# Attention and a channel-mix layer on one core: when the second stage's weights are loaded, and in which memory

## The chip, the core and the metric

One core of one Trainium2 chip runs the kernel. The metric is the device time of one execution in microseconds (us). PE is TensorE (matmul), DVE is VectorE, ACT is ScalarE, POOL is GpSimd, and SP only issues transfers (DMAs); ACT issues some as well. A difference of 0.2% is about what a measurement of this kernel can tell from none.

## The reference, cut to what matters

```python
scores = 30 * tanh((q @ k.T) / sqrt(64) / 30)          # 8 batches x 12 heads, 448 x 64
attn   = softmax(scores) @ v                            # -> x: 8 x 448 x 768
xk = mu_k * x + (1 - mu_k) * x_prev                     # x_prev: the token before
xr = mu_r * x + (1 - mu_r) * x_prev
k  = maximum(xk @ w_k, 0)                               # 768 -> 1024, "the keys"
out = sigmoid(xr @ w_r) * ((k * k) @ w_v)               # 768 -> 768, 1024 -> 768
```

Everything is float32. A float32 product is made of three matmuls of a faster type: each operand is split into a high part (a copy in that type) and a low part (the operand less its high part).

## The kernel before

**First stage.** Two heads are a pair; 48 pairs, six to a batch. For each pair PE makes the scores, ACT takes tanh and exp, DVE sums the rows, PE multiplies by v. The row sums go to DRAM and back (`gather`, `recip`, `rec_store`, `rec_load`), then DVE normalizes (`norm`, L382), and DVE, ACT and POOL make xk and its high and low parts (`x_high`, `x_low`). The keys of a batch are 8 columns of w_k (`fc`) by 6 pairs (`dc`) by 3 matmuls = 144 matmuls of 448 columns, dealt out among the later pairs' work (`K`). From pair 14 on two pairs make one `unit`, and the string `UNIT` lists in which order the program writes out their work. Each engine takes its own instructions in that order.

**The passage.** After the last pairs, 36 key matmuls of batch 6 and all 144 of batch 7 are left. The pools of attention are closed, and seven weight groups are prepared: `group_load` reads two blocks of w_r or w_v from DRAM into a staging tile (`stg`, two buffers), `group_sums` makes four sums and differences of their quarters (POOL, but group 0 on DVE), `group_split` makes the high part of seven quarters by ACT (L107, 2688 columns) and the low part by DVE (L577), and then loads the group after next. `TAIL` says which of this follows which eighth of batch 7's keys. Two banks hold the keys on their way from PE to `relu` (ACT, L454). The mixing of xr (`mix_r`, L615 and L616) and its first sum (`sum1`, L634) follow the keys.

**Second stage.** 14 blocks of 256 tokens, each a run `r` and a run `v`, each run seven products of a Strassen-like scheme (L661; 9 matmuls of 384 columns in `r`, 12 in `v`). A table of slots (`PRODUCTS`, `runs`) interleaves them: the first is r's product 4, then r's 2, 3 and 0, then v's 4, then r's 5. Product 3 adds to the bank of product 4, after ACT has copied that bank out (L672).

Of the kernel before, what the change touches and what calls it, by code (L numbers as in the profile page):

```python
# [19 lines left out]
DF = 1024  # L20
# [36 lines left out]
TAIL = ("d0 s0", "p1", "s1 p2", "s2", "p3", "s3 p4", "s4 p5", "p6")  # L57
# [20 lines left out]
k_store k_store f x_high.1 x_low.1 weight_store load_vl load_v.1 x_store.0 weight_load load_qk.1 x_store.1"""  # L78

# [9 lines left out]
class Body:  # L89
# [26 lines left out]
    def consts(self, pool):  # L116
        nc = self.nc
        self.cap_t = pool.tile([P, 1], F32, name="cap_t")
        nc.sync.dma_start(self.cap_t, self.cap.to_broadcast([P, 1]))
        self.scl_t = pool.tile([P, 1], F32, name="scl_t")  # L120
        nc.vector.reciprocal(self.scl_t, self.cap_t)
        nc.vector.tensor_scalar(self.scl_t, self.scl_t, D ** -0.5, None, op0=ALU.mult)
        self.mu, self.om = {}, {}
        for n, src in (("k", self.muk), ("r", self.mur)):
            m = pool.tile([P, ND], F32, name="mu_" + n)
            nc.sync.dma_start(m, src)
            o = pool.tile([P, ND], F32, name="om_" + n)
            nc.vector.tensor_scalar(o, m, -1.0, 1.0, op0=ALU.mult, op1=ALU.add)
            self.mu[n], self.om[n] = m, o
        self.grd = pool.tile([P, 1], F32, name="grd")  # L130
        if self.maxima:
            nc.vector.memset(self.grd, 1e-9)
            return
        sq = pool.tile([1, 1], F32, name="sq")
# [37 lines left out]
    def init_attn(self):  # L172
        self.raw, self.QK, self.rawv, self.S, self.P32, self.PV, self.R, self.rs = ({} for _ in range(8))
        self.M, self.SUM = {}, {}
        self.one = self.rawp.tile([P, 64], F32, name="one", bufs=1)
        self.nc.gpsimd.memset(self.one, 1.0 / 32)
# [9 lines left out]
    def load_v(self, i):  # L186
        t = self.rawv[i] = self.rawp.tile([P, 3, 2, D], F32, name="rv")
        w = 6 * D
        self.nc.sync.dma_start(t.rearrange("p c h d -> p (c h d)"),
                               self.v[i // NP, i % NP // 2][:, i % 2 * w:i % 2 * w + w])  # L190

    def load_vl(self, i):
        t = self.rawv[i, "L"] = self.rawp.tile([P, 2, D], F32, name="rvl")
        self.nc.sync.dma_start(t.rearrange("p h d -> p (h d)"), self.v[i // NP, i % NP // 2][:, 12 * D:])
# [361 lines left out]
    def group_load(self, k):  # L556
        p, g = self.group(k)
        c = g if p == "r" else ND + g
        w = self.stg.tile([P, 7, HN], F32, name="stg", tag=f"stg{k % 2}")
        for j in range(2):  # L560
            self.nc.sync.dma_start(w[:, 2 * j:2 * j + 2].rearrange("p a e -> p (a e)"), self.w_d[c + j * KG[p]])
        self.W[k] = w
# [10 lines left out]
    def group_split(self, k):  # L573
        p, g = self.group(k)
        w, (hi, lo) = self.W.pop(k), self.WS[p, g]
# [5 lines left out]
    def weight_tiles(self, pool, p, gs):  # L581
        w = pool.tile([P, len(gs), 2, 7, HN], F32R, name="w2" + p, align_bytes=256)
        for j, g in enumerate(gs):
            self.WS[p, g] = w[:, j, 0], w[:, j, 1]

    def tail_work(self, h):
        for op in TAIL[h].split():
            if op[0] in "dp":
                self.group_sums(int(op[1]), "v" if op[0] == "d" else "p")
            else:  # L590
                self.group_split(int(op[1]))


    def load_x(self, c):
# [3 lines left out]
        xc = self.XC = self.xin.tile([P, ND, CH + 2], F32, name="xc")  # L598
# [46 lines left out]
    def split(self, p, c, m):  # L645
        a = self.block(p, c, m)
        hi, lo = (self.opp[p].tile([P, KG[p], P], F32R, name=p + t, align_bytes=256) for t in "hl")
# [64 lines left out]
    def chain(self, pe, prep, s0, s1):  # L712

        for s in range(s0, s1):
            if s in pe:
                self.product(*pe[s])
            for fn, a in prep.pop(s, []):
                fn(*a)
# [3 lines left out]
    def step(self, i):  # L722
# [19 lines left out]
        for op in (UNIT if unit else START_EVEN if even else START_ODD).split():  # L742
            g, j1 = (), 0
            if "." in op:
                op, j1 = op[:-2], int(op[-1])
            if op[-1] in "012L" and op not in ("L", "VL", "OL"):
                op, g = op[:-1], (op[-1] if op[-1] == "L" else int(op[-1]),)
            if op in pair:
# [14 lines left out]
                if 0 <= j < NPAIR and op not in (late if j in ONES else first) and not (uncut(j) and op in ('qk_high', 'qk_low')):  # L763
                    getattr(self, name.get(op, op))(j, *g)
            elif op == "K":
# [27 lines left out]
    def run(self):  # L793
# [8 lines left out]
        with ExitStack() as outer:  # L802
# [10 lines left out]
            kst, hst, est, wst, ast, sst, pst = (ExitStack() for _ in range(7))  # L813
# [4 lines left out]
            self.WKH, self.WKL = ([w.tile([P, ND, DF // 2], F32R, name=n, align_bytes=256) for w in (wk0, wk1)]  # L818
                                  for n in ("wkh", "wkl"))
            self.ps_k = pool("ps_k", 2, pst, space=PSUM)  # L820
# [3 lines left out]
            sump = pool("sump", 1, ast, **right)  # L824
            self.up = pool("up", 2, ast, **right)
            self.rawp = pool("rawp", 2, ast, **right)
            self.qp = pool("qp", 3, ast, **right)
# [3 lines left out]

            self.init_x(self.up)
# [8 lines left out]
            for i in range(NSTEP):  # L841
# [4 lines left out]
                if i == NPAIR + 1:  # L846
# [4 lines left out]
                    for st in (wst, est, ast, sst, pst):  # L851
                        st.close()
                    self.W, self.WS, self.A, self.S1, self.OP, self.bank, self.RS = ({} for _ in range(7))
                    self.weight_tiles(pool("w2r", 1, **right), "r", range(3))
                    self.opp = {"r": pool("opr", 3, **right)}
                    self.xin = pool("xin", 1, **right)
                    self.stg = pool("stg", 1, **right)
# [4 lines left out]
                    self.ps_k = pool("ps_k", 2, pst, space=PSUM)  # L862
                    self.ps_2 = pool("ps_2", 1, space=PSUM, **right)
                if i <= NPAIR:
                    self.step(i)
                if i > NPAIR + 1:
                    for h in range(2):
                        n = B * NF * ND * 3 - (2 * (NSTEP - i) - h) * 3 * ND
# [3 lines left out]
                        h += 2 * (i - NPAIR - 2)  # L872
                        if h == 4:
                            hst.close()
                            self.weight_tiles(pool("w2v0", 1, **right), "v", range(2))
                        self.tail_work(h)
# [5 lines left out]
            self.weight_tiles(pool("w2v1", 1), "v", range(2, 4))  # L882
            self.rsp, self.opp["v"] = pool("rsp", 1), pool("opv", 3)
            self.chain(pe, prep, -12, -6)
            self.group_split(6)
            self.CP = self.stg.tile([P, 7, HN], F32, name="cp", tag="stg0")
            self.chain(pe, prep, -6, -3)
            self.group_split(5)
            t = self.stg.tile([P, 7 * HN], F32, name="x1", tag="stg1")
            self.kr1 = t[:, 0:NF * CH].rearrange("p (c s) -> p c s", c=NF)  # L890
            self.S1["v"] = t[:, NF * CH:NF * CH + KG["v"] * P].rearrange("p (c s) -> p c s", c=KG["v"])
            self.chain(pe, prep, -3, max(pe) + 1)
# [52 lines left out]
```

## Time and profile before

| | us |
|---|---|
| median of 3 runs | 942.55 (941.82 to 942.9) |
| the profiled execution | 943.12 |
| its span | 941.3 |
| PE busy | 893.2 (95%) |
| DVE, ACT, POOL busy | 733.2, 620.8, 423.4 |

A span is cut in windows, and each window lists how long each engine was busy in it, and the clock that PE was granted (1.00 is 2.4 GHz, 0.50 is 1.2 GHz). A timeline row is a start, a duration, an engine with the line, what is written from what, and in brackets the idle time before it and the engine that ended it. PE's rows overlap their successors, so the distance between starts is what a matmul costs.

### The profile page before, as it was taken

How to read it: one execution, taken by the hardware profiler on the slowest of the kernel's cores; microseconds unless marked ns; L12 is line 12 of the kernel's file. 1: busy time of each engine (PE TensorE's matmuls, PEld its weight loads, DVE VectorE, ACT ScalarE, POOL GpSimd, SP SyncE). 2: the span in 40 equal slices, each digit the busy share in tenths (PEclk: the TensorE clock that was granted, in tenths of full speed). 3: DMA queues.
4: the chain of work that ended last, by engine and by line, in shares of the span. 5: the costliest groups of instructions: out<-in, count | busy, mean ns of one | idle time of the engine just before them, and what ended most of it. 6: DMA issues, size and time to landing. Idle time of an engine off the chain costs nothing.

```text
span 941.3 us, 14302 instructions
## 1 busy us (share of the span) xinstructions
PE 893.2 (95%) x5046; PEld 700.4 (74%) x5046; DVE 733.2 (78%) x1088; ACT 620.8 (66%) x957; POOL 423.4 (45%) x412
## 2 busy tenths in 40 slices
PE   7999999999999999999999638999999999999996
PEld 2334556667777676777669538999999999999996
DVE  5778997777888888878874368888888888888873
ACT  7888878787887887877863346554554555555542
POOL 2433364456556546455534853333433334333440
PEclk9999999999999999999999959999999999999999
DMA  7446655657776656666638422323332233323301
GB/s 249 122 150 183 193 172 171 185 164 200 216 207 195 196 172 187 204 207 195 183 111 274 142 77 88 104 80 111 104 113 93 80 104 113 105 88 102 113 26 46
DMA packets 96410, 137.06 MB, mean 146 GB/s; under 512 B 11464, under 2 KB 84936, under 8 KB 96328
## 3 DMA queue, kind: packets, MB, share of 16 engines
q1 hardware_dynamic: 87112, 121.37, 42.1%
q10 hardware_dynamic: 9216, 14.68, 4.2%
q8 instruction: 41, 0.67, 0.3%
q14 instruction: 41, 0.34, 0.1%
HBM read 91.23 MB, written 42.38 MB: 142 GB/s over the span
## 4 chain that ended last, share of the span: by engine, by line
PE 50%; DVE 22%; ACT 13%; issue 7%; DMA 4%; POOL 3%; SPq 1%; ACTq 0%; POOLq 0%; DVEq 0%
PE kps L444 20%; PE pv L285 11%; PE s L250 10%; DVE vl L649 3%; DVE cp L692 3%; DVE t L616 3%; ACT vh L107 3%; DVE rl L649 3%; PE ps2a L661 2%; PE pv L294 2%; PE s L260 2%; ACT t L615 2%; ACT rh L107 2%; DVE x L621 2%; DVE kr L621 2%
## 5 line engine op out<-in xcount | busy, mean ns | idle before, releaser
L266 ACT ACTIVATE p<-s,scl_t 128x896 f32<-128x896 f32 x144 | 139.2, 996 | 16.0 <-PE s L250 14.8
L444 PE MATMUL kps<-xkh,wkl 128*128 128x448 f32 x384 | 144.4, 376 | 4.1 <-ACT ko L454 4.1
L276 ACT ACTIVATE p<-p,cap_t 128x896 f32<-128x896 f32 x144 | 145.2, 1036 | 1.9
L331 DVE TRANSPOSE_TENSOR_REDUCE r<-p 128x28 f32<-128x896 f32 x126 | 136.2, 1093 | 7.6 <-ACT p L276 7.6
L444 PE MATMUL kps<-xkl,wkh 128*128 128x448 f32 x384 | 141.4, 368 | 0.0
L444 PE MATMUL kps<-xkh,wkh 128*128 128x448 f32 x384 | 141.1, 368 | 0.0
L526 POOL TENSOR_TENSOR wsq<-wa,wsq 128x384 f32<-128x384 f32 x44 | 47.1, 1071 | 157.6 <-DVE wsq L519 157.6
L285 PE MATMUL pv<-p,rv 128*64 128x448 f32 x576 | 115.1, 545 | 0.0
L661 PE MATMUL ps2a<-w2v,vh 128*128 128x384 f32 x448 | 88.5, 339 | 8.3 <-DVE cp L691 8.3
L444 PEld LDWEIGHTS kps<-xkh,wkl 128*128 128x128 f32 x384 | 72.1, 188 | 30.8 <-issue 13.7
L285 PEld LDWEIGHTS pv<-p,rv 128*64 128x64 f32 x576 | 38.6, 136 | 66.5 <-issue 55.8
L661 PEld LDWEIGHTS ps2a<-w2v,vh 128*128 128x128 f32 x448 | 77.8, 188 | 13.0 <-DVE cp L691 11.0
L444 PEld LDWEIGHTS kps<-xkl,wkh 128*128 128x128 f32 x384 | 72.2, 188 | 9.1 <-issue 2.8
L444 PEld LDWEIGHTS kps<-xkh,wkh 128*128 128x128 f32 x384 | 72.1, 188 | 6.5
L382 DVE TENSOR_TENSOR x<-pv,r 128x448 f32<-128x448 f32 x48 | 28.2, 620 | 55.0 <-DMA r<-rec_d 54.8
L649 DVE TENSOR_TENSOR rl<-t,rh 128x384 fp32r<-128x384 f32 x70 | 39.7, 567 | 39.1 <-ACT rh L107 38.2
L113 POOL TENSOR_TENSOR qkl<-rqk,qkh 128x832 fp32r<-128x832 f32 x34 | 67.5, 1986 | 2.7
L661 PE MATMUL ps2a<-w2r,rh 128*128 128x384 f32 x336 | 68.2, 338 | 0.2 <-ACT rh L107 0.2
L649 DVE TENSOR_TENSOR vl<-x,vh 128x512 fp32r<-128x512 f32 x63 | 56.1, 898 | 13.9 <-ACT vh L107 13.7
L661 PEld LDWEIGHTS ps2a<-w2r,rh 128*128 128x128 f32 x336 | 59.7, 190 | 0.8 <-ACT rh L107 0.8
L616 DVE SCALAR_TENSOR_TENSOR t<-xc,mu_r,t 128x256 f32<-128x256 f32 (+3 forms) x120 | 56.8, 526 | 1.1 <-ACT t L615 0.3
L113 POOL TENSOR_TENSOR xkl<-xk,xkh 128x448 fp32r<-128x448 f32 x48 | 55.3, 1152 | 3.9
(125 smaller groups left out, 1903.5 us busy)
## 6 DMA issues: line engine op xcount, KB each, us to landing
rqk<-qk SPq DMA_DIRECT2D x47, 448.0 KB
k_d<-ko ACTq DMA_DIRECT2D x64, 224.0 KB
x_d<-x SPq DMA_DIRECT2D x48, 224.5 KB
out<-cp SPq DMA_DIRECT2D x56, 192.0 KB
rv<-v SPq DMA_DIRECT2D x48, 192.0 KB
r<-rec_d SPq DMA_DIRECT2D x36, 224.0 KB
kr<-k_d SPq DMA_DIRECT2D x7, 1024.0 KB
x<-k_d SPq DMA_DIRECT2D x7, 1024.0 KB
```

Source lines behind the costliest of these rows:

```text
L107: self.nc.scalar.copy(out, x)
L113: {"p": self.nc.gpsimd, "v": self.nc.vector}[e].tensor_sub(*a)
L250: nc.tensor.matmul(s[:, h, 0:S], qk[a][p, k], qk[b][p, 0:S], start=(n == 0), stop=(n == len(terms) - 1))
L266: self.nc.scalar.activation(p32, self.S.pop((i, g))[:, :, 0:S], AF.Tanh, scale=self.scl_t)
L276: self.nc.scalar.activation(p32, p32, AF.Exp, scale=1.0 if self.maxima else self.cap_t)
L285: nc.tensor.matmul(pv[p, 0:S], v[:, g, h, :], ph[:, h, :], start=(g == 0), stop=False)
L331: self.nc.vector.tensor_reduce(out=r1[:, :, 3 if g == "L" else g], in_=self.P32[i, g].rearrange("p h (b k) -> p (h b) k", k=32), axis=mybi ...
L444: nc.tensor.matmul(self.kps[fc][:, 0:S], w, m[:, dc, :], start=first, stop=last)
L526: {"p": self.nc.gpsimd, "v": self.nc.vector}[e].tensor_add(sq, f(a), sq)
L616: nc.vector.scalar_tensor_tensor(out=td, in0=self.XC[:, d, j0 + o + 1:j1 + o + 1], scalar=self.mu["r"][:, d:d + 1], in1=td, op0=ALU.mult, ...
L649: self.nc.vector.tensor_sub(lo, a, f(hi))
L661: self.nc.tensor.matmul(o, a[:, g], self.WS[p, g][w][:, m], start=first and part == 0 and g == 0, stop=last and part == 2 and g == KG[p] - ...
```

## The change

Attention's tiles and those that live longer now stand in separate pools (`ast`, `lst`); the first is closed inside the last unit, right after its last matmuls with v, and the tiles of the second stage (`w2A` to `w2O`, one of 10.5 KB per partition each) wait for the old tiles that they lie on, one by one. Groups 0, 1 and 2 are loaded, summed and split within the last unit (`LAST`, in which `l`, `p` or `d`, `c`, `s` are load, sums on POOL or DVE, high, low). A low part goes into a slot whose raw group is done with. `mix_r` and `sum1` of the first block move among batch 7's keys (`@` in `TAIL`). Batch 7's first four columns take pairs 0 to 3 first and pairs 4 and 5 later, and each of its eight columns has a bank of its own. The tile sizes and two pads put every tile of the first stage on a multiple of 64 bytes; in the program before most lay 32 bytes off.

```diff
-TAIL = ("d0 s0", "p1", "s1 p2", "s2", "p3", "s3 p4", "s4 p5", "p6")
+TAIL = ("p3 s2 @-12 @-11 @-10", "p4 c3 s3", "p5 @-9", "open c4 s4 @-8 c5", "p6", "@-7 @-6", "@-5 @-4", "")
+TAIL_TAGS = ("c0", "b0", "a0", "c1", "b1", "a1")
+LAST = """V.0 V.1 VL next gather f f f p0 recip weight_load rec_store f f weight_rest weight_sum rec_load l2 d1 c0 s0
+norm.0 norm.1 K K K relu K relu k_store c1 mix_old.0 mix_new.0 x_high.0 x_low.0 s1 weight_low f K K mix_old.1 relu
...
@@ key_order
+        if b == B - 1:
+            early = [x for x in t[:4 * n] if x[1] < 4]
+            return early + [x for x in t[:4 * n] if x[1] >= 4] + t[4 * n:]
@@ kpart
-                if self.ps_k is not None:
+                if self.ps_2 is not None and fc > 1:
+                    self.kps[fc] = self.ps_2.tile([P, 512], F32, name="kps", tag="ps2" + TAIL_TAGS[fc - 2])
+                elif self.ps_k is not None:
@@ group_split
-        self.copy("s", hi, w)
-        self.nc.vector.tensor_sub(lo, w, f(hi))
-        if k + 2 < KG["r"] + KG["v"]:
-            self.group_load(k + 2)
+    def group_high(self, k):
+        hi = self.weight_tile(HIGH[k], F32R)
+        self.WS[self.group(k)] = [hi, None]
+        self.copy("s", hi, self.W[k])
+    def group_low(self, k):
+        pair = self.WS[self.group(k)]
+        pair[1] = self.weight_tile(LOW[k], F32R)
+        self.nc.vector.tensor_sub(pair[1], self.W.pop(k), f(pair[0]))
@@ run
+            def open_first():
+                ast.close()
+                self.weight_slots(pool("w2a", 1, **tile_wise), "EGDFHBCA")
+                for k in range(2):
+                    self.group_load(k)
...
-                    for k in range(2):
+                    for k in (3, 5):
                         self.group_load(k)
-                    pe, prep = self.runs()
-                    self.chain(pe, prep, -40, -12)
+                    self.preps(-23)
+                    self.group_load(4)
+                    self.preps(-16)
...
-            self.chain(pe, prep, -12, -6)
-            self.group_split(6)
...
+            self.tail_work("s5 c6")
+            self.chain(pe, -6, -1)
+            self.prep[-1].reverse()
+            self.preps(-1)
+            self.tail_work("s6")
```

On SP, from the last stores of x of the unit before to the last weight load: `sq<-r` is the gather of the row sums, `r<-rec_d` the return of the reciprocals, `xc` and `kr` the second stage's x and keys. Before:

```order
L361 DMA sq_171<-r_170 32x224 x4
L373 DMA rec_d_88<-rs_5110 28x2x32
L378 DMA r<-rec_d_88 64x2x448 x2
L546 DMA w_d<-wsq 128x384
L415 DMA x_d<-x_140 128x449
L415 DMA x_d<-x_142 128x449
L561 DMA stg<-w_d 128x768 x4
L599 DMA xc<-x_d 128x6x257
L603 DMA kr<-k_d 128x8x256
L561 DMA stg<-w_d 128x768 x10
```

Now:

```order
L576 DMA w2A<-w_d 128x768 x2
L576 DMA w2C<-w_d 128x768 x2
L371 DMA sq_179<-r_178 32x224 x4
L383 DMA rec_d_88<-rs_5160 28x2x32
L388 DMA r<-rec_d_88 64x2x448 x2
L576 DMA w2E<-w_d 128x768 x2
L561 DMA w_d<-wsq 128x384
L425 DMA x_d<-x_147 128x449
L425 DMA x_d<-x_149 128x449
L576 DMA w2I<-w_d 128x768 x2
L576 DMA w2H<-w_d 128x768 x2
L634 DMA xc<-x_d 128x6x257
```

Groups 0 and 1 now stand ahead of the gather, and group 2 right behind the return; groups 4 and 6 (`w2K`, `w2M`) and two more loads follow these rows.

On POOL, the last pairs' x parts, the weight sums (`stg`) and the first block's sums (`s`). Before:

```order
L526 TENSOR_TENSOR wsq<-wa,wsq 128x384
L103 TENSOR_SCALAR xkh<-xk 128x448
L113 TENSOR_TENSOR xkl<-xk,xkh 128x448
L103 TENSOR_SCALAR xkh<-xk 128x448
L113 TENSOR_TENSOR xkl<-xk,xkh 128x448
L113 TENSOR_TENSOR stg<-stg 128x384 x24
L879 TENSOR_LOAD flag
L634 TENSOR_TENSOR s_5510<-t 128x384
```

Now:

```order
L122 TENSOR_TENSOR w2A<-w2A 128x384 x4
L541 TENSOR_TENSOR wsq<-wa,wsq 128x384
L112 TENSOR_SCALAR xkh<-xk 128x448
L122 TENSOR_TENSOR xkl<-xk,xkh 128x448
L112 TENSOR_SCALAR xkh<-xk 128x448
L122 TENSOR_TENSOR xkl<-xk,xkh 128x448
L122 TENSOR_TENSOR w2I<-w2I 128x384 x4
L122 TENSOR_TENSOR w2K<-w2K 128x384 x4
L122 TENSOR_TENSOR w2H<-w2H 128x384 x4
L669 TENSOR_TENSOR s_5374<-t 128x384
L122 TENSOR_TENSOR w2M<-w2M 128x384 x4
L122 TENSOR_TENSOR s_5374<-s_5374,t 128x384
```

Twelve weight sums instead of 24 stand between the last x part and the first sum of the block.

On ACT, around the last keys (`ko<-kps`): `w2..` and `w2v` are high parts of weights, `ro` and `rh` those of the block, `cp<-ps2c` the copy of the first product's bank. Before:

```order
L107 CAST w2v<-stg 128x2688
L454 ACTIVATE ko<-kps 128x448
L460 DMA k_d<-ko 128x448
L879 TENSOR_LOAD flag
L615 ACTIVATE t<-xc,om_r 128x256 x6
L107 CAST rh<-s_5510 128x384
L107 CAST w2v<-stg 128x2688
L107 CAST rh<-t 128x384
L672 COPY cp<-ps2c 128x384
```

Now:

```order
L116 CAST ro<-s_5374 128x384
L116 CAST w2K<-w2H 128x2688
L469 ACTIVATE ko<-kps 128x448
L475 DMA k_d<-ko 128x448
L469 ACTIVATE ko<-kps 128x448
L475 DMA k_d<-ko 128x448
L116 CAST ro<-t 128x384
L469 ACTIVATE ko<-kps 128x448
L475 DMA k_d<-ko 128x448
L116 CAST ro<-t 128x384
L469 ACTIVATE ko<-kps 128x448
L475 DMA k_d<-ko 128x448
```

The first product's operand (`s`) is split ahead of four relus and their stores; behind these rows stand the flag, the last group's high part (`w2O`) and then the copy `cp<-ps2c`.

## Rows read from the trace of the kernel before

**Rows 1.** Windows: us; busy time (and count) of each engine; PEclk, DMA share, GB/s.

```profile
200.00:300.00 100.00, 99.97 (x610) 69.82 (x609) 83.98 (x115) 82.18 (x101) 56.52 (x57) 1.00 0.66 198
...
500.00:520.00 20.00, 20.00 (x99) 18.14 (x98) 10.13 (x8) 8.28 (x9) 13.21 (x9) 1.00 0.91 302
...
540.00:560.00 20.00, 5.17 (x15) 4.65 (x15) 11.68 (x10) 8.64 (x12) 13.70 (x11) 0.52 0.29 94
...
600.00:700.00 100.00, 97.86 (x558) 96.18 (x557) 83.59 (x130) 54.63 (x128) 36.91 (x30) 1.00 0.29 92
```

**Rows 2.** Waits of PE in 484 to 582, the longest: us in total, times, longest.

```profile
PE ps2c L661 <- ACT rh L107: 20.6, 2, 19.7
```

**Rows 3.** Timeline of PE: last keys and first products.

```profile
494.36 0.47 PE L444 MATMUL kps<-xkh,wkl 128*128 128x448 f32 x1
...
526.73 0.48 PE L444 MATMUL kps<-xkh,wkl 128*128 128x448 f32 x1 [2.47 <-ACT ko L454]
527.04 0.37 PE L444 MATMUL kps<-xkl,wkh 128*128 128x448 f32 x1
...
534.02 0.37 PE L444 MATMUL kps<-xkh,wkh 128*128 128x448 f32 x1
554.07 2.29 PE L661 MATMUL ps2c<-w2r,rh 128*128 128x384 f32 x6 [19.68 <-ACT rh L107]
...
573.30 1.20 PE L661 MATMUL ps2a<-w2r,rh 128*128 128x384 f32 x6
574.34 0.68 PE L661 MATMUL ps2a<-w2r,rl 128*128 128x384 f32 x3
```

**Rows 4.** Timeline of ACT in the passage.

```profile
539.56 2.43 ACT L107 CAST w2v<-stg 128x2688 fp32r<-128x2688 f32 x1 [6.19 <-POOL stg L113]
541.90 0.54 ACT L454 ACTIVATE ko<-kps 128x448 f32<-128x448 f32 x1
542.47 0.33 ACTq L460 DMA_DIRECT2D k_d<-ko  x1
...
553.50 0.51 ACT L107 CAST rh<-s 128x384 fp32r<-128x384 f32 x1 [7.60 <-POOL s L634]
...
559.57 0.48 ACT L672 COPY cp<-ps2c 128x384 f32<-128x384 f32 x1 [2.80 <-DVE w2v L577]
```

**Rows 5.** Timeline of POOL: an x part, weight sums beside DVE's subtraction, and alone.

```profile
503.89 1.15 POOL L113 TENSOR_TENSOR xkl<-xk,xkh 128x448 fp32r<-128x448 f32 x1
...
510.64 3.62 POOL L113 TENSOR_TENSOR stg<-stg 128x384 f32<-128x384 f32 x1
...
549.51 3.01 POOL L113 TENSOR_TENSOR stg<-stg 128x384 f32<-128x384 f32 x3 [0.22 <-DMA stg<-w_d]
```

**Rows 6.** Timeline of DVE in the passage.

```profile
498.46 1.16 DVE L382 TENSOR_TENSOR x<-pv,r 128x448 f32<-128x448 f32 x2 [5.48 <-DMA r<-rec_d]
499.87 0.68 DVE L402 SCALAR_TENSOR_TENSOR xk<-x,mu_k,pv 128x448 f32<-128x448 f32 x1 [0.25 <-ACT pv L397]
502.47 0.68 DVE L402 SCALAR_TENSOR_TENSOR xk<-x,mu_k,pv 128x448 f32<-128x448 f32 x1 [1.93 <-POOL xkl L113]
...
542.02 2.96 DVE L577 TENSOR_TENSOR w2v<-stg,w2v 128x2688 fp32r<-128x2688 f32 x1 [5.37 <-ACT w2v L107]
...
554.05 0.56 DVE L649 TENSOR_TENSOR rl<-s,rh 128x384 fp32r<-128x384 f32 x1 [4.47 <-ACT rh L107]
...
562.16 2.28 DVE L621 TENSOR_TENSOR kr<-kr 128x2048 f32<-128x2048 f32 x1
```

**Rows 7.** Timeline of SP's issues.

```profile
480.01 0.86 SPq L415 DMA_DIRECT2D x_d<-x  x2
486.34 2.46 SPq L361 DMA_DIRECT2D sq<-r  x4
...
513.41 32.40 SPq L561 DMA_DIRECT2D stg<-w_d  x10
```

**Rows 8.** Windows, a short one: PE's clock after its last key.

```profile
538.00:540.00 2.00, 0.00 (x0) 0.00 (x0) 0.00 (x0) 0.44 (x1) 1.54 (x3) 0.68 0.90 323
```

More of the change, by code (lines that the diff above doesn't have):

```diff
@@ L130, in consts @@
         self.grd = pool.tile([P, 1], F32, name="grd")
+        sq = pool.tile([1, 1], F32, name="sq")
+        pool.tile([P, PAD[0]], F32, name="pad_left")
         if self.maxima:
@@ L174, in init_attn @@
         self.M, self.SUM = {}, {}
-        self.one = self.rawp.tile([P, 64], F32, name="one", bufs=1)
+        self.one = self.vp.tile([P, 64], F32, name="one", bufs=1)
         self.nc.gpsimd.memset(self.one, 1.0 / 32)
@@ L186, in load_v @@
     def load_v(self, i):
-        t = self.rawv[i] = self.rawp.tile([P, 3, 2, D], F32, name="rv")
+        t = self.rawv[i] = self.vp.tile([P, 3, 2, D], F32, name="rv")
         w = 6 * D
@@ L192, in load_vl @@
     def load_vl(self, i):
-        t = self.rawv[i, "L"] = self.rawp.tile([P, 2, D], F32, name="rvl")
+        t = self.rawv[i, "L"] = self.vp.tile([P, 2, D], F32, name="rvl")
         self.nc.sync.dma_start(t.rearrange("p h d -> p (h d)"), self.v[i // NP, i % NP // 2][:, 12 * D:])
@@ L571, in group_sums, with weight_slots, weight_tile, tail_work @@
         self.sub(e, t4, b21, t2)
-    def group_split(self, k):
-        p, g = self.group(k)
-        w, (hi, lo) = self.W.pop(k), self.WS[p, g]
-        self.copy("s", hi, w)
-        self.nc.vector.tensor_sub(lo, w, f(hi))
-        if k + 2 < KG["r"] + KG["v"]:
-            self.group_load(k + 2)
[L581 to L589, printed above, removed]
-            else:
-                self.group_split(int(op[1]))
+    def group_high(self, k):
[6 more added lines that the diff above has]
+        self.nc.vector.tensor_sub(pair[1], self.W.pop(k), f(pair[0]))
+    def weight_slots(self, pool, slots):
+        for c in slots:
+            self.slot[c] = pool
+            self.weight_tile(c, F32 if c in RAW_SLOTS else F32R)
+            if c in RAW_SLOTS:
+                self.W[RAW_SLOTS.index(c)] = self.held[c]
+    def weight_tile(self, c, dt):
+        if c in self.slot:
+            self.held[c] = self.slot[c].tile([P, 7, HN], dt, name="w2" + c, tag="w2" + c)
+        return self.held[c]
+    def tail_work(self, ops):
+        for op in ops.split():
+            if op[0] == "@":
+                self.preps(int(op[1:]))
+            elif op == "open":
+                self.open_second()
+            else:
+                k = int(op[1])
+                fn, a = dict(l=(self.group_load, ()), d=(self.group_sums, "v"), p=(self.group_sums, "p"),
+                             c=(self.group_high, ()), s=(self.group_low, ()))[op[0]]
+                fn(k, *a)
+    def preps(self, slot):
+        assert min(self.prep, default=slot) >= slot
+        for fn, a in self.prep.pop(slot, []):
+            fn(*a)
     def load_x(self, c):
@@ L646, in split @@
         a = self.block(p, c, m)
-        hi, lo = (self.opp[p].tile([P, KG[p], P], F32R, name=p + t, align_bytes=256) for t in "hl")
+        pools = self.opp[p]
+        pools.append(pools.pop(0))
+        t = pools[-1].tile([P, 2, KG[p], P], F32R, name=p + "o")
+        hi, lo = t[:, 0], t[:, 1]
         self.copy("s", hi, a)
@@ L710, in runs, with chain @@
         return pe, prep
-    def chain(self, pe, prep, s0, s1):
+    def chain(self, pe, s0, s1):
         for s in range(s0, s1):
@@ L716, in chain @@
                 self.product(*pe[s])
-            for fn, a in prep.pop(s, []):
-                fn(*a)
+            self.preps(s)
             if s in pe:
@@ L741, in step @@
         seen = {}
-        for op in (UNIT if unit else START_EVEN if even else START_ODD).split():
+        for op in (LAST if i == NPAIR else UNIT if unit else START_EVEN if even else START_ODD).split():
             g, j1 = (), 0
+            if len(op) == 2 and op[0] in "lpdcs":
+                self.tail_work(op)
+                continue
             if "." in op:
@@ L812, in run @@
             cpool = pool("cpool", 1)
-            kst, hst, est, wst, ast, sst, pst = (ExitStack() for _ in range(7))
+            pool("pad_right", 1, **right).tile([P, PAD[1]], F32, name="pad_right")
+            kst, hst, est, wst, lst, ast, sst, pst = (ExitStack() for _ in range(8))
             wk1 = pool("wk1", 1, kst)
@@ L817, in run @@
             wk0 = pool("wk0", 1, hst)
-            self.WKH, self.WKL = ([w.tile([P, ND, DF // 2], F32R, name=n, align_bytes=256) for w in (wk0, wk1)]
+            self.WKH, self.WKL = ([w.tile([P, ND, DF // 2], F32R, name=n) for w in (wk0, wk1)]
                                   for n in ("wkh", "wkl"))
-            self.ps_k = pool("ps_k", 2, pst, space=PSUM)
+            self.ps_k, self.ps_2 = pool("ps_k", 2, pst, space=PSUM), None
             self.ps_t, self.ntile = None, 0
@@ L830, in run, with open_second @@
             self.ps_s = pool("ps_s", 2, sst, space=PSUM, **right)
+            def open_first():
[3 more added lines that the diff above has]
+                    self.group_load(k)
+            def open_second():
+                hst.close()
+                self.weight_slots(pool("w2c", 1, **tile_wise), "L")
+                self.weight_slots(pool("stage", 1, est, **tile_wise), "M")
+                self.group_load(6)
+            tile_wise = dict(right, reuse_waits="tile")
+            self.open_first, self.open_second = open_first, open_second
+            self.slot, self.held = {}, {}
+            self.W, self.WS, self.A, self.S1, self.OP, self.bank, self.RS = ({} for _ in range(7))
             self.init_x(self.up)
@@ L850, in run @@
                     assert not self.full and not self.done
-                    for st in (wst, est, ast, sst, pst):
+                    for st in (lst, wst, est, sst, pst):
                         st.close()
[L853 to L857, printed above, removed]
-                    for k in range(2):
-                        self.group_load(k)
-                    pe, prep = self.runs()
-                    self.chain(pe, prep, -40, -12)
-                    self.ps_k = pool("ps_k", 2, pst, space=PSUM)
-                    self.ps_2 = pool("ps_2", 1, space=PSUM, **right)
+                    self.opp = {"r": [pool("opr", 3, **tile_wise)]}
+                    self.xin = pool("xin", 1, **tile_wise)
+                    self.weight_slots(pool("w2b", 1, **tile_wise), "KJI")
+                    pe, self.prep = self.runs()
+                    for k in (3, 5):
+                        self.group_load(k)
+                    self.preps(-23)
+                    self.group_load(4)
+                    self.preps(-16)
+                    self.ps_k = pool("ps_k", 2, pst, space=PSUM, reuse_waits="tile")
+                    self.ps_2 = pool("ps_2", 1, space=PSUM, **tile_wise)
                 if i <= NPAIR:
@@ L866, in run @@
                 if i > NPAIR + 1:
-                    for h in range(2):
-                        n = B * NF * ND * 3 - (2 * (NSTEP - i) - h) * 3 * ND
+                    for h in range(2 * (i - NPAIR - 2), 2 * (i - NPAIR - 1)):
+                        n = B * NF * ND * 3 - (8 - h) * 3 * ND
                         self.kpart(n, n + 3 * ND)
@@ L871, in run @@
                         self.k_store()
[L872 to L876, printed above, removed]
+                        self.tail_work(TAIL[h])
             self.k_store()
```

37 lines of the change are left out of this document (23 added, 14 removed).

## The prediction

> **What bounds the kernel now.** I read the windows first: in the first stage PE is busy 99.97 of 100 us, in the second 97.86 of 100, both at full clock; in 540 to 560 it is busy 5.17 of 20 at a mean clock of 0.52 [rows 1]. So PE sets the pace on both sides of one hole, and the hole is what there is to win. The waits name it: of 20.6 us that the first products wait for ACT's high part, 19.7 are one wait [rows 2]. The timeline then gives the places [rows 3]: 180 key matmuls are left at 494.36; a wait of 2.47 for `relu` (two banks) stands before the one at 526.73; the last starts at 534.02 and ends its turn at 534.23; the first product starts at 554.07; and only from r's product 5, at 573.30, PE runs without gaps. The last step back is to see why the wait was so long: ACT's `rh` waited 7.60 for POOL's `s` and stands at 553.50 [rows 4], and `s` stands behind the 24 weight sums that POOL ends at 552.5 [rows 5]. So the hole comes from POOL's order, not from its speed: it is busy 56.52 of 100 us in the first stage.
>
> From 573.30 on, the order of every engine is what it was, and PE is the bound [rows 1]. So the change is worth the amount by which r's product 5 comes earlier, plus what the first stage gives. I work that out in the times of the profiled execution (943.12), and take the difference from the median (942.55); the two differ by 0.06%.
>
> **The change, step by step.**
>
> *Loads ahead of the gather.* SP is free at 480.87, and the gather stood at 486.34 [rows 7]. Four loads of 384 KB (1.57 MB) go out before it; at the 302 GB/s that the core moved in 500 to 520 [rows 1] they need 5.2 us, from about 481, so they are through at about 486.3. I cost them at nothing. What hides a small delay: `norm` ends at 499.6 [rows 6], the last x part at 505.0 [rows 5], and now DVE's first split (2.96, [rows 6]) comes between, so the last ends near 508. PE needs pairs 4 and 5 only after 36 + 48 = 84 matmuls, at 494.36 + 84 x 0.205 = 511.6. The cover is some 3 us; past it PE waits one for one.
>
> *Eight banks.* They take the 2.47 away, and the slow restart with it: the matmul after it came 0.31 later where 0.205 is the rule ((534.02 - 527.04)/34, [rows 3]). The keys end at 534.23 - 2.5 = 531.7.
>
> *The chain to the first product.* `sum1` on POOL now stands behind 12 weight sums instead of 24. A sum takes 1.0 alone (3.01 for three), but one beside a DVE subtraction took 3.62 [rows 5], about the subtraction's own time: the two engines take turns. From about 509, when the x parts are through: 12 x 1.0, three subtractions of 2.96 and `sum1` itself 1.0 make 21.9, so 530.9. ACT's high part 0.51 [rows 4] and DVE's low part 0.56 [rows 6] then give a first product at about 532.3, just behind the last key.
>
> *The first two products.* A product of r is 9 matmuls of 0.173 ((574.34 - 573.30)/6, [rows 3]) = 1.6, or 1.8 with its start. The first ends at 534.1. The second waits for its operand, which POOL sums behind group 6's four sums, 4 x 1.0 and a part lost to a subtraction: it runs from about 536.3 to 538.2.
>
> *The third product waits anew.* Its bank is the first product's, and ACT must copy it out (0.48, [rows 4]). Ahead of that copy ACT now has, from about 531, two high parts of 2.43, four `relu`s and their stores (0.54 + 0.33), the operands of the block, and a wait for POOL's sums of group 6 and of the third operand: 530.9 + 6 x 1.0 + one subtraction's 1.1 left over = 538.0. Behind that stand that operand's high part 0.51, the last relu and store 0.87, a flag that I put at 0.5, the last group's high part 2.43 and the copy: 542.8, say 543.2 with the hand-overs. So PE idles some 5 us there. Products 3 and 4 run to 546.7. Product 4 of v then wants the last low part. On DVE that is, from about 543: `square` 2.28, a subtraction 2.96, two lows of 0.56 and the last subtraction 2.96 [rows 6] = 9.3, so 552.3; five matmuls of 0.173 that need it follow, and r's product 5 starts at 553.2. That is 573.30 - 553.2 = 20.1 earlier.
>
> *The clock.* After its last key PE's granted clock stood at a mean of 0.68 in 538 to 540, four to six us after the idling began [rows 8], and at 0.52 in 540 to 560 [rows 1]. In the new hole (two pieces of 2 and 5 us) it may fall as well. If all of products 3 and 4 and v's ran at the lower level, they would take twice their 5.4 us or so; since part of it lies under DVE's chain in any case, I put the loss between 0 and 4 and take 1.5. Passage: 20.1 - 1.5 = 18.6. The Trainium skill ("TensorE: Matmul & The Clock Gate", section "What's actually happening") says that the throttled state is the default and that activity releases it; by that rule a hole filled in time loses no clock at all, and the sum would be 20.1; the 0.68 of the trace agrees with its fall.
>
> *Weight slots.* The second stage's weights and operands now lie in slots that change hands. The one place where that adds a wait in every run is v's third split, which reuses the buffer of product 6; it is a rival below. I cost it at nothing.
>
> *Where the tiles lie.* The key operands move from 32 bytes off to a multiple of 64. A key matmul of 448 columns takes 0.2053, a product's of 384 columns, whose operands already lie on 64, 0.1733 [rows 3]. In proportion 448 columns would take 0.2022, so 8 x 144 = 1152 key matmuls pay 3.1 ns each, 3.6 us, that the column count does not explain. With a fixed excess over the 2.4 GHz time (0.1733 - 0.160 = 0.0133) they would take 0.200, and pay 6.1 us. If the place of the tiles is the cause, the first stage gives 3.6 to 6.1 back, as PE is its bound; if it is not, 0. Against it: on DVE `mix_new` took 0.68 from a tile 32 bytes off and 0.68 from one on 64 [rows 6]. A slowdown I exclude. Between 0 and 6.1 I take 2, a little over half of the proportional price.
>
> Sum: 18.6 + 2.0 = 20.6; 942.55 - 20.6 = **922.0** (922.5 beside the profiled execution).
>
> **The rivals.**
>
> *Earlier (E).* POOL isn't held up by DVE's three subtractions: `sum1` comes at 522 instead of 531, the sums of group 6 with it, the copy some 6 us sooner, and the last low part too; with the full price for the tiles, 18.6 + 6 + 4 = 28.6, so 914. For it: a sum alone takes 1.0. Against: the 3.62 [rows 5].
>
> *Late loads (C).* The 1.57 MB delay the gather, so that `norm` and the x parts come more than 3 us late, or the late loads (some 4 MB behind the x stores) keep POOL waiting; group 6 and all behind it slide by 10. Then the gain is 8 to 10: 933. For it: the DMA share is 0.91 in 500 to 520 already [rows 1], and 3 us of cover is little. Against: SP stood in waits through 32.40 us of its issues [rows 7], so the queue as such had room. The Trainium skill ("DMA: Bandwidth & Descriptors", section "Two DMAs through the same engine are not ordered") says that within one queue of one engine descriptors start in order; by that the gather starts only behind the loads, here at about 486.3, where it stood already.
>
> *No effect (N).* The freed tiles wait for the old pool as a whole, the loads go out where they did, and only the banks help: 942.55 - 2.5 + 1 = 941. The order of SP speaks against it.
>
> *Slower (S).* v's third split waits on ACT, in all 13 later runs, for product 6 to leave its buffer, and PE stands behind it: at worst one v product, 12 x 0.173 = 2.1 us, per run, 13 x 2.1 = 27, less 18.6 = 8.4 lost, so 951. It decides from 18.6/13 = 1.4 us per run. Against: PE's 97.86 of 100 [rows 1] shows operands that come well ahead.
>
> **How the numbers follow.** Forecast 0.66, with a range of its own of 916 to 928: below it the full price of the tiles (4 more than taken) and 2 of clock; above it no gain from the tiles (2), 2.5 more of clock and 1.5 of DVE. E 0.13 (914, from 909), C 0.12 (933, to 937), N 0.03, S 0.06 (951). The range 912 to 933 leaves out half of C, N, S and a little of E, about 0.17. A change within 0.2%, what a measurement can tell from none, is 0.03: N. Slower by more, 0.06: S. Faster 0.91.
>
> **What the new profile would show.** Right: no wait of keys on `ko`, the last key near 531.7 and the first product within 1.5 us of it; a wait of about 5 us of `ps2c` on ACT's `cp`, behind the last group's high part; r's product 5 at 551 to 556; POOL's sums of 3 to 4 us wherever DVE subtracts; the clock below 1.00 only in 540 to 555. The spacing of key matmuls settles the tiles: 205 ns or 200 to 202. Wrong: PE waiting for pair 4's or 5's x parts near 511 (C), for `vo` in each run (S), or a first product not before 540.

## The result, and the profile after

The changed kernel takes 925.95 us (925.59 to 926.25, 4 runs), the kernel before 942.24 beside it: 16.3 us less, a ratio of the two times of 0.9826 with a 95% interval of 0.9809 to 0.9843. Forecast were 922.0 and a range of 912 to 933. The profiled execution has a span of 923.9, against 941.3. Of all executions below one, of the kernel that moves group 6's sums, was in a slow state (1103 us at a granted clock of 0.75), and its ratio leaves it out.

The windows of the passage (columns as in [rows 1]): where PE was busy 5.17 of 20 us in 540 to 560, it now is for 12.89. The one hole has become the four waits listed below, in two windows with a mean clock of 0.79 each.

```profile
500.00:520.00 20.00, 20.00 (x99) 18.34 (x99) 15.55 (x14) 10.69 (x15) 17.06 (x12) 1.00 0.79 286
520.00:540.00 20.00, 14.27 (x58) 12.62 (x56) 12.98 (x8) 8.22 (x10) 18.65 (x13) 0.79 0.59 201
540.00:560.00 20.00, 12.89 (x59) 11.94 (x59) 17.90 (x19) 12.03 (x24) 10.83 (x4) 0.79 0.03 12
```

The four longest waits of PE in 470 to 600 (us in total, times, longest), in place of the 19.7 of [rows 2]:

```profile
PE ps2c L699 <- ACT ro L116: 4.8, 2, 4.3
PE ps2c L699 <- ACT cp L710: 4.0, 1, 4.0
PE ps2c L699 <- DVE w2H L595: 3.0, 1, 3.0
PE ps2b L699 <- ACT ro L116: 1.4, 1, 1.4
```

PE's timeline shows the last key, the first matmul of r's products 4, 2 and 3, the one of v's product 4 that waits for its low weights, and the first of r's product 5:

```profile
527.71 0.37 PE L459 MATMUL kps<-xkh,wkh 128*128 128x448 f32 x1
532.37 0.69 PE L699 MATMUL ps2c<-w2B,ro 128*128 128x384 f32 x1 [4.29 <-ACT ro L116]
...
537.06 0.69 PE L699 MATMUL ps2b<-w2B,ro 128*128 128x384 f32 x1 [1.44 <-ACT ro L116]
...
544.33 0.69 PE L699 MATMUL ps2c<-w2B,ro 128*128 128x384 f32 x1 [4.02 <-ACT cp L710]
...
553.83 0.44 PE L699 MATMUL ps2c<-w2H,vo 128*128 128x384 f32 x1 [2.95 <-DVE w2H L595]
...
554.82 0.33 PE L699 MATMUL ps2a<-w2B,ro 128*128 128x384 f32 x1
```

For a count that does not depend on the first stage I take three marks in PE's timeline: the 180th key matmul from the end, r's product 5, and the last matmul.

| | before | after | gained |
|---|---|---|---|
| start to 180th key from the end | 494.36 | 491.21 | 3.15 |
| from there to r's product 5 | 78.94 | 63.61 | 15.33 |
| from there to the last matmul | 362.04 | 362.78 | -0.74 |

### The profile page after: what moved, and what is told of

The parts are those of the page before. It is cut to its first block, busy times and chain, and to the rows that moved or that the text cites. A ratio compares the mean times of both kernels' runs of the same rounds, so it can differ in the third digit from the quotient of the medians.

```text
span 923.9 us, 14292 instructions
## 1 busy us (share of the span) xinstructions
PE 889.7 (96%) x5046; PEld 698.6 (76%) x5046; DVE 742.4 (80%) x1092; ACT 620.9 (67%) x957; POOL 424.3 (46%) x408
## 4 chain that ended last, share of the span: by engine, by line
PE 53%; DVE 21%; ACT 12%; issue 7%; POOL 5%; DMA 2%; ACTq 0%; SPq 0%; POOLq 0%; DVEq 0%
PE kps L459 21%; PE pv L295 11%; PE s L260 11%; DVE vo L687 3%; DVE cp L730 3%; ACT vo L116 3%; DVE ro L687 3%; DVE t L651 3%; PE pv L304 2%; PE ps2a L699 2%; PE s L270 2%; ACT ro L116 2%; ACT t L650 2%; DVE x L656 2%; POOL t L122 1%
## 5 line engine op out<-in xcount | busy, mean ns | idle before, releaser
L541 POOL TENSOR_TENSOR wsq<-wa,wsq 128x384 f32<-128x384 f32 x44 | 47.4, 1076 | 155.5 <-DVE wsq L534 155.5
L687 DVE TENSOR_TENSOR ro<-t,ro 128x384 fp32r<-128x384 f32 x70 | 40.6, 580 | 43.1 <-ACT ro L116 42.1
L687 DVE TENSOR_TENSOR vo<-x,vo 128x512 fp32r<-128x512 f32 x63 | 56.1, 898 | 14.8 <-ACT vo L116 14.5
L651 DVE SCALAR_TENSOR_TENSOR t<-xc,mu_r,t 128x256 f32<-128x256 f32 (+3 forms) x120 | 59.3, 546 | 0.9
L721 ACT ACTIVATE rs<-rs 128x384 f32<-128x384 f32 x28 | 14.7, 526 | 61.2 <-DVE rs L720 61.2
L112 POOL TENSOR_SCALAR qkh<-rqk 128x832 fp32r<-128x832 f32 x34 | 30.6, 900 | 45.1 <-DMA rqk<-qk 41.1
L669 POOL TENSOR_TENSOR s<-t 128x384 f32<-128x384 f32 x14 | 16.9, 1207 | 73.9 <-DVE t L651 73.9
L116 ACT CAST ro<-t 128x384 fp32r<-128x384 f32 x70 | 34.4, 509 | 20.3 <-POOL t L122 19.9
```

Source lines behind the costliest of these rows:

```text
L112: self.nc.gpsimd.tensor_scalar(out, x, 1.0, 0.0, op0=ALU.mult, op1=ALU.add)
L116: self.nc.scalar.copy(out, x)
L541: {"p": self.nc.gpsimd, "v": self.nc.vector}[e].tensor_add(sq, f(a), sq)
L651: nc.vector.scalar_tensor_tensor(out=td, in0=self.XC[:, d, j0 + o + 1:j1 + o + 1], scalar=self.mu["r"][:, d:d + 1], in1=td, op0=ALU.mult, ...
L687: self.nc.vector.tensor_sub(lo, a, f(hi))
```

## The experiments

Each kernel is the changed one with the edit shown, timed beside the kernel before on one chip. The "mark" is the 180th key from the end, and the "passage" is the second row of the table, from the mark to r's product 5.

**Where the key operands lie.** 32 bytes ahead of `xkp0` and of `xkp1` put half the moving operands and half of w_k off.

```diff
+            xkp1.tile([P, 8], F32, name="off1")
+            self.xkp[0].tile([P, 8], F32, name="off0")
```

> The changed kernel with 32 bytes put ahead of the key operands of either parity of batches, which by the way the memory is dealt leaves half of the moving key operands and half of w_k's tiles 32 bytes off a multiple of 64; nothing else differs. Theory 'tiles': a key matmul takes 205 ns where its moving operand lies off, 202.7 where not, whatever w_k's place; 576 x 2.4 ns = 1.4, so 927.3. Rival 'not the tiles' (the faster keys come from what else runs beside them): 202.7 everywhere, 926.0.

Measured 925.71, ratio 0.9826 (0.9812 to 0.9841). The time can't tell the two theories apart, but the matmuls can. I took the distance between the starts of consecutive key matmuls, sorted by where the program places their two operands, counted in 128 bytes (means of 260 to 279 distances each): moving 64 and w_k 0, 200.1 ns; 32 and 32, 202.6; 32 and 0, 204.2; 64 and 32, 205.6. In the change both lie at 0: 202.9; before, 32 or 96 against 0: 205.1. So the place counts, but it is the place of both operands together, and w_k's counts as much as the moving one's (205.6 against 200.1 where only w_k's differs); "a multiple of 64" was the wrong rule. My expectation for w_k's place was a miss.

**All key operands 64 apart.** Pads of 64 bytes stand ahead of `xkp0`, `xkp1` and half of w_k.

> The changed kernel with all moving key operands at 64 and all of w_k at 0, counted in 128 bytes (both at 0 in the change, 32 or 96 against 0 before). Theory 'distance' (from the run with half of the operands 32 bytes off: 200.1 ns where the two operands of a matmul lie 64 apart, 202.6 where 0, 204.2 to 205.6 where 32): 200.1 for all 1152 key matmuls, 2.8 ns less each, 3.2 us, all of it carried: 922.7. Rival 'chance of one run': 202.9 and 926.0.

Measured 925.92, ratio 0.9818 (0.9798 to 0.9837): no gain that can be told, and a miss. The pads had left the distance at 64 only when counted in 128 bytes; counted in 256 bytes half of the keys were at 64 (200.0 and 200.3 ns) and half at 192 (202.2 and 202.3). And the scores between took 101.6 us in all where they had taken 99.9, which ate up what the keys saved. Of these 1.7 us, 1.1 are one wait of a score for `relu`, at 200.71.

**The same for the second stage.** Pads of 64 bytes stand ahead of its operands.

> The changed kernel with pads of 64 bytes ahead of the second stage's operands, by which part of v's matmuls have weights and operand 64 apart (counted in 128 bytes) and the others 0. Theory 'distance', as for keys: 2 to 3 ns less where they are 64 apart, about half of v's 1176 matmuls, 1.2 to 1.8 us: 924.5. Rival 'already at its best' (the excess over 384 columns at 2.4 GHz is 13.4 ns, what keys 64 apart have over theirs): 173.4 everywhere, 926.0.

Measured 926.89, ratio 0.9830 (0.9815 to 0.9845). Its matmuls took 173.5 to 174.3 ns with the operand at 0 or 128 of 256 bytes, and 175.6 to 176.2 with it at 64; in the change, with everything at 0, they take 173.5. So 64 costs some 2 ns here where it saved them for the keys: 'distance' missed, and no place that was tried is better than the change's.

**The gather ahead of the loads.**

```diff
-... next gather f f f p0 ... l2 d1 c0 s0 norm.0 norm.1
+... next gather l0 l1 f f f p0 ... l2 d1 c0 norm.0 norm.1 s0
...
-                for k in range(2):
-                    self.group_load(k)
```

> The changed kernel with the loads of groups 0 and 1 issued behind the gather, and group 0's subtraction behind norm. Theory 'gather': the loads ahead of it held the row sums up by 4 us; norm comes some 4 us earlier, the last x part and the first product with it, 922 to 924. Rival 'port': DVE and POOL take turns, and their joint work between here and v's first product is what sets the end; group 0's sums then start 4 us later in a stretch that has no slack, and nothing is won or up to 4 lost, 926 to 930.

Measured 926.99, ratio 0.9832 (0.9818 to 0.9845). The row sums were back 3.9 us after the gather's issue, as before, where the change needs 7.9 (483.29 to 491.15). `norm` came 6.2 us behind the mark, where the change has 8.3. But the return of the reciprocals now stood behind the loads, group 0's sums began at 491.5 and not at 485.7, and its subtraction (2.95) now stood between `norm` and the x parts, so that the last x part ended 18.3 us after the mark (17.9 in the change). So the loads do hold the row sums up by 4 us, as 'gather' had it, but this order wins nothing. What the order of the transfers is worth without moving the subtraction was not tested.

**Two banks for the last four columns.**

```diff
-                if self.ps_2 is not None and fc > 1:
+                if self.ps_2 is not None and fc in (2, 3):
```

> The changed kernel with the last four key columns back in two banks. Theory 'port': the first product waits for POOL's sum and not for PE, and the wait of 4.3 us ahead of it takes in whatever the keys lose (up to 2.5): 926.0, within 0.4. As the prediction priced the banks: 2.5 slower, 928.4.

Measured 933.51, ratio 0.9900 (0.9884 to 0.9915): 7.6 slower than the change's 925.95, and both theories missed. ACT's timeline of this kernel shows why:

```profile
515.72 2.42 ACT L116 CAST w2J<-w2I 128x2688 fp32r<-128x2688 f32 x1
518.04 0.53 ACT L469 ACTIVATE ko<-kps 128x448 f32<-128x448 f32 x1
...
522.05 2.43 ACT L116 CAST w2L<-w2K 128x2688 fp32r<-128x2688 f32 x1 [0.84 <-ACT ko L469]
531.82 0.51 ACT L116 CAST ro<-s 128x384 fp32r<-128x384 f32 x1 [7.33 <-POOL s L669]
532.24 2.43 ACT L116 CAST w2K<-w2H 128x2688 fp32r<-128x2688 f32 x1
534.57 0.54 ACT L469 ACTIVATE ko<-kps 128x448 f32<-128x448 f32 x1
```

A `relu` that frees a bank now stands behind the work on weights: the one at 518.04 behind the high part `w2J`, the one at 534.57 behind `ro`, which waits 7.33 for POOL, and the high part that follows it. PE waits 4.49 and 6.40 for them at 518.63 and 535.16, and some 15 keys behind each wait start 0.37 apart, at half clock. The keys take 53.2 us in place of 36.5, and the waits that follow can cover only 9 of these 16.7. A missing bank cost a wait of 2.5 us in the order of before; the banks of the last four columns are worth 7.6 in the new one.

**The key order undone.**

```diff
-        if b == B - 1:
+        if b == B:
```

> The changed kernel with batch 7's columns in the plain order, pairs 4 and 5 not put back. PE then needs the last pairs' x parts at about 501 and they are ready at 506 and 509: it waits some 8 us among the keys. Theory 'port': the 4.3 us ahead of the first product take in half, so 4 slower, 930. If that wait is no cover: 934. If the order is worth nothing: 926.

Measured 925.86, ratio 0.9820 (0.9807 to 0.9833): the number of an order that is worth nothing, where 'port' had 930. PE waits 5.0 us among the keys for x parts and not at all ahead of the first product, which comes 46.0 us behind the mark and not 41.2. But r's product 5 comes only 0.9 later: the passage is 64.5. So the waits ahead of the first products are a cover, as 'port' had it, and it takes in nearly all of the 4.9 us, where 'port' had half.

**Fewer sums ahead of the first product.** `group_sums` of group 3 is three copies on ACT; four of POOL's twelve sums are left out.

> The changed kernel without group 3's four sums on POOL (ACT makes three copies in their place, so part of v's weights are not what they should be; left out are 4 of 12 sums ahead of the block's first). Theory 'port': the first product comes about 4 us earlier, right behind the last key, and as DVE and POOL have that much less to do, v's product 4 and r's product 5 too: 922. Rival 'order': the first product comes earlier, but v's product 4 waits for its own row (square, the last two subtractions, v's first sum), which starts when it did: 925.5 to 926.

Measured 923.77, ratio 0.9809 (0.9796 to 0.9822); the changed kernel on the same chip 925.61. The first product comes 1.0 earlier than there (530.57 against 531.53) and not 4: POOL could not begin earlier by the whole of the four sums, as the next group's load had not landed:

```profile
506.99 1.33 POOL L122 TENSOR_TENSOR xkl<-xk,xkh 128x448 fp32r<-128x448 f32 x1
512.88 6.27 POOL L122 TENSOR_TENSOR w2K<-w2K 128x384 f32<-128x384 f32 x4 [4.56 <-DMA w2K<-w_d]
519.12 7.20 POOL L122 TENSOR_TENSOR w2H<-w2H 128x384 f32<-128x384 f32 x4
526.27 3.71 POOL L673 TENSOR_TENSOR s<-t 128x384 f32<-128x384 f32 x1
```

But the 1.0 us by which the block's first sum came earlier (526.27 against 527.23 in the change repeated on this chip) is there again in r's product 5 (553.02 against 554.24), and the medians differ by 1.84. From the first product to r's product 5 it takes 22.45 us, as in the change, where 'order' would have made this stretch longer. So the chain from the last x part over POOL's sums carries through to the end, and v's product 4 has no start of its own.

**The order behind it.** Three kernels change only the order of the last group's work. The first puts its subtraction ahead of the small low parts:

```diff
-            self.tail_work("s5 c6")
+            self.tail_work("s5 c6 s6")
```

> The changed kernel with DVE's last weight subtraction (w2H of group 6) right behind that of group 5, ahead of the small low parts. Theory 'order on DVE': v's product 4 waits for that subtraction, which ended at 553.8 because it stood behind waits; it ends near 549, r's product 5 comes some 2.5 earlier, 923.5. Rival 'port': what is put back (two low parts of r, one of v) is needed just as soon, and the end moves by less than 0.5: 925.5 to 926.5.

Measured 926.03, ratio 0.9818 (0.9803 to 0.9834): the executions lie between 923.86 and 926.65, and no gain can be told. In the profile, which is that of the fastest, the passage is 61.1, 2.5 shorter as expected, and 0.5 of that is lost again behind r's product 5 (363.3 to the last matmul, 362.8 in the change). The second moves group 6's sums behind the block's:

```diff
-... "p6", "@-7 @-6", "@-5 @-4", "")
+... "", "", "", "")
+            self.tail_work("s5 @-7 @-6 @-5 @-4 p6")
+            self.chain(pe, -6, -5)
+            self.tail_work("c6 s6")
```

> The changed kernel with the passage in another order: behind the last relus group 5's subtraction, then the block's second and third operand, and only then group 6's sums; the copy of product 4's bank ahead of group 6's high part; its subtraction right behind it. Theory 'order': the waits of 1.4, 4.0 and 3.0 us ahead of r's 2, 3 and v's 4 came from the rows that stood ahead and not from the amount of work; DVE was idle for 3.9 us at 533 to 537 and 1.7 at 538 to 540, POOL for 3.5 at 539 to 543; r's product 5 comes 4 to 6 earlier, 920 to 922. Rival 'port': the joint work of DVE and POOL fills the stretch, and the end moves by less than 1: 925 to 927.

Measured 928.89 to 932.89, ratio 0.9868 (0.9845 to 0.9891): slower than the change, a miss. The block's second operand now stood behind four relus on ACT (539.40 where it had been 536.50), POOL's next sum waited 5.33 for it, and group 6's high part 5.42 for POOL. The third kernel goes back to the old order of POOL, and puts the copy ahead of the high part:

```diff
-            self.tail_work("s5 c6")
-            self.chain(pe, -6, -1)
+            self.tail_work("s5")
+            self.chain(pe, -6, -5)
+            self.tail_work("c6")
+            self.chain(pe, -5, -1)
+            self.tail_work("s6")
```

> The changed kernel with ACT's copy of product 4's bank ahead of group 6's high part, and DVE's last weight subtraction ahead of v's and r's later low parts but behind those of r's products 0 and 5. Theory 'order': the third product's wait of 4.0 us shrinks to 1.2 (the copy at 541 and not 543.8), and v's product 4 does not wait for the subtraction; from the 180th key matmul from the end to r's product 5 it takes 60 to 61 us, where the change took 63.6: 922.5 to 923.5. Rival 'port': the pair's joint work sets it, 63 or more, and 925.5 to 926.5.

> The changed kernel itself, once more, on the chip of the others of this call: 925.9, and 63 to 64 us from the 180th key matmul from the end to r's product 5.

Measured 923.82, ratio 0.9803 (0.979 to 0.9817), against 925.61, ratio 0.9828 (0.9814 to 0.9841), for the change on the same chip. The passage is 61.0 against 63.1, as 'order' had it. But not for the reason given: the copy came at 543.31 and not at 541,

```profile
541.28 0.33 ACTq L475 DMA_DIRECT2D k_d<-ko  x1
543.31 0.48 ACT L710 COPY cp<-ps2c 128x384 f32<-128x384 f32 x1 [2.06 <-DMA k_d<-ko]
543.68 2.44 ACT L116 CAST w2O<-w2M 128x2688 fp32r<-128x2688 f32 x1
```

since its tile lies where, by the program's addresses, the last stores of the keys are still read. What is won is mostly the subtraction's place on DVE, as in the first of the three: PE waits 1.3 for it and not 3.3. Of the 2.1 us, 1.1 are lost again behind r's product 5 (363.85 to the last matmul against 362.76), where PE waits 1.1 for v's operand. So the marks leave 1.0 of the 1.8 by which the medians differ; the rest is not explained by this order.

**Both together.** This order is joined with pads that put all moving key operands at 64 and w_k at 0 of 256 bytes.

> The order of the kernel with the copy first, and pads that put all moving key operands at 64 and all of w_k at 0, counted in 256 bytes. Theory 'distance': all 1152 key matmuls take 200.1 ns (202.9 in the change); up to the last 180 they save 2.7 us; with the order 919.5 to 921. Rival: the scores between take longer by what the keys save, as they did by 1.8 us in the run with half of the keys at that distance: 922 to 923.5.

Measured 922.12, ratio 0.9786 (0.9772 to 0.9799): 3.5 below the change on the same chip, the fastest of all, and the number of the rival. PE's timeline of its last keys, (526.08 - 524.08)/10 = 0.200:

```profile
524.08 0.36 PE L459 MATMUL kps<-xkl,wkh 128*128 128x448 f32 x1
...
526.08 0.36 PE L459 MATMUL kps<-xkh,wkh 128*128 128x448 f32 x1
530.38 0.44 PE L699 MATMUL ps2c<-w2B,ro 128*128 128x384 f32 x1 [3.95 <-ACT ro L116]
```

All keys take 200.1 ns, as 'distance' had it; the 180th from the end starts at 490.16, 1.0 earlier than in the repeated change (491.12). Keys next to keys saved 2.0 us up to there (195.4 to 193.4), and the scores gave 0.9 back. Of that, 0.5 is one wait of a score for `relu`, at 343.30, like the 1.1 in the run with half of the keys at 64; where the rest comes from was not found out. The passage is 60.1.

## Why the prediction was right, and where it was off

The sum was 20.6 us; the marks give 3.15 + 15.33 - 0.74 = 17.7, the medians 16.3. (The profiled execution of the kernel before took 943.12, 0.9 more than the median of 942.24.)

What was right is what the change is about: POOL's order. The sum for the first product started 47.4 us behind the end of the last x part (505.04) in the kernel before:

```profile
552.48 0.99 POOL L634 TENSOR_TENSOR s<-t 128x384 f32<-128x384 f32 x1
```

It now starts 19.0 us behind it (509.11 to 528.08). No run takes the weight groups alone back into the passage, so their share of the 15.3 us is read from these rows and not tested.

- *The first product* is the step that failed. It was to follow the last key's end by 0.6 us and came 4.5 behind it, or 41.2 us behind the mark (491.21 to 532.37) where the forecast had 37.9 (494.36 to 532.3): 3.3 too few, the whole shortfall of the passage. The term was the loads ahead of the gather, which I had costed at nothing: groups 0 and 1 were to be loaded, summed and subtracted within the wait for the row sums. But the row sums took 4 us longer from the gather's issue to their use (483.29 to 491.15, 7.9 for 3.9; in 484 to 486 the DMA engines were busy at a share of 0.99, where it had been 0.00, and with the gather ahead of the loads it was 3.9 again), `norm` came 8.3 us behind the mark and not 4.1, and the last x part was through 17.9 behind it (509.1) where I had taken 14.6 (509, but with PE 3 us later). On SP and DVE the gather and the use of the row sums were, before and now:

```profile
486.34 2.46 SPq L361 DMA_DIRECT2D sq<-r  x4
490.22 1.07 DVE L365 TENSOR_REDUCE sr<-sq 32x56 f32<-32x896 f32 x1 [0.57 <-DMA sq<-r]
...
483.29 6.47 SPq L371 DMA_DIRECT2D sq<-r  x4
491.15 1.07 DVE L375 TENSOR_REDUCE sr<-sq 32x56 f32<-32x896 f32 x1 [2.80 <-DMA sq<-r]
```

POOL's timeline then shows sums at 4.7 to 7.2 us for four:

```profile
507.78 1.33 POOL L122 TENSOR_TENSOR xkl<-xk,xkh 128x448 fp32r<-128x448 f32 x1
509.07 4.70 POOL L122 TENSOR_TENSOR w2I<-w2I 128x384 f32<-128x384 f32 x4
513.72 7.23 POOL L122 TENSOR_TENSOR w2K<-w2K 128x384 f32<-128x384 f32 x4
520.91 7.20 POOL L122 TENSOR_TENSOR w2H<-w2H 128x384 f32<-128x384 f32 x4
528.08 3.70 POOL L669 TENSOR_TENSOR s<-t 128x384 f32<-128x384 f32 x1
```

and DVE's timeline shows its work beside them:

```profile
513.33 3.26 DVE L595 TENSOR_TENSOR w2C<-w2E,w2F 128x2688 fp32r<-128x2688 f32 x1 [2.51 <-ACT w2F L116]
516.51 7.04 DVE L651 SCALAR_TENSOR_TENSOR t<-xc,mu_r,t 128x256 f32<-128x256 f32 x6
523.47 3.77 DVE L595 TENSOR_TENSOR w2E<-w2I,w2J 128x2688 fp32r<-128x2688 f32 x1
527.33 3.60 DVE L595 TENSOR_TENSOR w2I<-w2K,w2L 128x2688 fp32r<-128x2688 f32 x1
```

From the last x part to the end of `s` it took 22.7, forecast were 21.9. One sum beside each subtraction (the third is `s` itself) took 3.6 to 3.75 us and the others 1.0 to 1.3, much as forecast; the six rows of `mix_r` on DVE (L651), which I had left out, cost POOL little, as the sums beside them took 1.1 to 1.2. So the length was right and the start was not: a step that was free for its own queue delayed what the next chain starts from. (The late-loads rival was this, at a smaller price and without PE waiting for x parts. Undoing the late gather won nothing in a run that also moved group 0's subtraction.)

- *From the first product to r's product 5* the forecast was 20.9 and 1.5 for the clock; it took 22.45. That the total fits is luck. The wait for `cp` was to be 5 and was 4.0. But the last low part, for which PE waits 2.95, ended at 553.8 and not at 552.3, and that is the 1.5: DVE's rows from `square` on took 13.2 us where I had 9.3, though they began at 540.6 and not at 543.

```profile
540.58 2.29 DVE L656 TENSOR_TENSOR kr<-kr 128x2048 f32<-128x2048 f32 x1
542.78 2.95 DVE L595 TENSOR_TENSOR w2N<-w2H,w2K 128x2688 fp32r<-128x2688 f32 x1
545.65 1.64 DVE L687 TENSOR_TENSOR ro<-t,ro 128x384 fp32r<-128x384 f32 x1
547.22 0.55 DVE L687 TENSOR_TENSOR ro<-s,ro 128x384 fp32r<-128x384 f32 x1
548.64 0.69 DVE L687 TENSOR_TENSOR vo<-x,vo 128x512 fp32r<-128x512 f32 x1 [0.88 <-ACT vo L116]
549.25 0.55 DVE L687 TENSOR_TENSOR ro<-t,ro 128x384 fp32r<-128x384 f32 x1
549.72 4.05 DVE L595 TENSOR_TENSOR w2H<-w2M,w2O 128x2688 fp32r<-128x2688 f32 x1
```

I had counted two low parts of 0.56, and the last subtraction at 2.96. The clock was 0.50 in the products from 532 to 548, from ahead of the first product on, and not only in 540 to 555. It can have cost the chain no more than the 0.88 that DVE waited at 548.64, as far as these rows show: ACT's `vo` stood behind the copy of a product that ran at half clock. In the run with fewer sums, whose first product ran at full clock, the stretch took 22.45 as well. By the Trainium skill ("TensorE: Matmul & The Clock Gate", section "What's actually happening") the throttled state is the default that activity releases; the trace agrees: after 4.3 us of waiting the first product's matmuls start 0.32 apart (532.86, 533.18), where 0.173 is the distance at full clock. Not every wait of this kind ends so: in the repeated change, after 3.7 us, they start 0.17 to 0.18 apart (531.99, 532.16).
- *Eight banks*: no key waits on `ko`; the keys take 36.7 us for 39.9. That was right, and in the new order the banks guard against three times as much.
- *Tiles*: 2.0 was taken from 0 to 6.1; the first stage gave 3.15, of which 2.9 are keys next to keys (198.05 to 195.16). That is 1.2 more than taken, within the range; the reason is the place of both operands and not the multiple of 64.
- *Key order*: its cover of x parts was costed at nothing; undone, it costs nothing that the time can tell.
- *Second stage*: costed at nothing; 0.74 were lost. In the first 10 us behind r's product 5 it was 0.9, with PE waiting 0.14 and 0.54 for operands that ACT makes; the blocks after that lose nothing more. v's split in its shared buffers (the slower rival) showed no wait.

## What to carry to other kernels

When work is moved into an engine's idle time, count what it delays for the chain that begins right behind it, and add up the moved work on engines that slow each other (here DVE and POOL) as one queue. A buffer whose lack costs a wait of 2.5 us in one order can be worth 7.6 in another: price it against what now stands ahead of the instruction that frees it. Once a hole is a chain, only what shortens the chain counts; the waits ahead of the first products swallowed a key order nearly whole. And a total that fits is not yet a sum that was right: here a longer chain on DVE stood in for a price of the clock.

## What was not expected of the hardware

A matmul of 448 columns takes from 200.1 to 205.6 ns by where its two operands lie in memory: best (200.0 to 200.3) where the moving one lies 64 bytes behind the stationary one, counted in 256 bytes; 202.2 to 202.9 at equal places and at 192; 204 to 206 where the two are 32 or 96 apart. A matmul of 384 columns in the second stage takes 173.5 with both operands at 0, and 2 to 3 ns more with its stationary operand at 64. The runs give these places and no rule that joins them.
